# Output copies ahead of filter work at block seams, and a new order of the filter loads, in a fused FFT filter and SwiGLU kernel

**Chip and metric.** One core of a Trainium2 chip. The time is device microseconds (us) of the whole program, as the median of several executions. The engines are TensorE (PE in the profile), VectorE (DVE), ScalarE (ACT), GpSimd (POOL) and SyncE (SP), which here only issues DMAs.

## The reference

Each of 8 sequences (3008 x 256) goes through a Fourier filter, and all tokens then go through a gated feed-forward layer:

```python
X = np.fft.rfft(x, axis=1)
y = np.fft.irfft(X * (filt_r + 1j * filt_i)[None], n=x.shape[1], axis=1)
# ... tokens: y as (24064, 256)
rms = np.sqrt(np.mean(y * y, axis=-1, keepdims=True) + 1e-06)
xn = y / rms * rms_g
g = xn @ w_gate
out = ((g * sigmoid(g)) * (xn @ w_val)) @ w_out     # d_ff 1536
```

## The kernel before

The FFT is done by matmuls with small tables. The feed-forward layer is a chain of 588 *slots*: a slot computes 128 of the 1536 hidden columns for 512 tokens. Twelve slots are a *block*, whose result collects in the two PSUM banks `po`. The filter work of the next sequence is spread over the slots of the one before, by the lists `pre`, `plan` and `late`. Sequence 0 has nobody to hide behind: its filter work is the *head*, some 47 us.

```python
stores = {}
for i in range(len(items) + 4):
    for fn, a in pre.get(i, ()):       # second products ("swap") of a filter unit
        fn(*a)
    if i < len(items):
        gv(*items[i])                  # 4 matmuls of 512 columns, silu on ACT, hh = pv * sg on DVE
    for fn, a in plan.get(i, ()):      # filter units, first and last products, norms
        fn(*a)
    if 2 <= i < len(items) + 2:
        down(*items[i - 2])            # 4 matmuls of 256 columns; at a block's end the copies of po
        # ... (cut)
    for fn, a in late.get(i, ()):
        fn(*a)
    # ... (cut)
```

A block ends at slots 13, 25, 37 and so on (slot % 12 == 1): there `down` also copies one `po` bank on ACT and the other on DVE, and the next slot's `down` writes both banks anew. This is the *seam*.

A filter unit of sequences 1 to 7 uses one PSUM bank, `psb`, of which there is only one:

```python
ps = bank(3 if b else (0, 3, 4, 5)[i % 4], "psb")           # two matmuls into it
nc.vector.tensor_tensor(out=s1, in0=ps, in1=f1, op=ALU.mult)  # L252
# swap_unit, first half (L278), then second half (L276), the last reader of psb:
nc.vector.scalar_tensor_tensor(out=s2[a], in0=ps[e], scalar=-1.0, in1=f2[e], ...)
nc.vector.tensor_tensor(out=s2[a], in0=ps[e], in1=f2[e], op=ALU.mult)
nc.gpsimd.tensor_tensor(out=s, in0=s1, in1=s2, op=ALU.add)    # L282
# ... (cut: units of sequence 1 that are not summed have two full products, L268 and L269)
```

The start of the head loads `x` on GpSimd's DMA queue, then the two filters:

```python
for c in range(NXC):
    x_load(0, c)                               # 8 DMAs on the GpSimd queue
nc.gpsimd.memset(fi[0][HALF:P], 0.0)
nc.gpsimd.memset(fr[0][0:HALF], 0.0)
# ... (cut)
for c in range(4):
    f_load(c, 0, nc.sync)                      # real filter
    f_load(c, 1, nc.gpsimd if c < 3 else nc.sync)   # imaginary filter
```

## Time and profile before

| | before |
|---|---|
| median of the first 3 executions | 893.95 us (893.05 to 894.44) |
| profiled execution, span of the core | 890.6 us |
| TensorE busy | 873.5 us, 98% |
| first gate matmul (end of the head) | 47.15 us |
| TensorE's waits after that | 4.3 us |

The page's busy row says which engine is the bound; the table of waits says how much of it can be won; a timeline around each wait says which instruction stood in the way. These lines are in the prediction below.

### The profile page before, as it was taken

The numbers are of one execution on the slowest core, as the hardware profiler recorded it, in microseconds if no ns is written. First come the engines' busy times: TensorE is split into PE (matmuls) and PEld (weight loads), VectorE is DVE, ScalarE is ACT, GpSimd is POOL, SyncE is SP. The second block draws the span as 40 slices with busy tenths as digits, with TensorE's granted clock in tenths as the row PEclk, the third lists the DMA queues.
The fourth block names the chain that finished last, engine by engine and source line by source line (L and its number), as shares of the span: only waits on it lengthen the run. The fifth ranks groups of instructions, "written<-read, shape, count | busy, mean of one in ns | idle before, by whom it ended". The sixth has DMA issues, their size and how long they took to land.

```text
span 890.6 us, 17468 instructions
## 1 busy us (share of the span) xinstructions
PE 873.5 (98%) x6258; PEld 559.4 (63%) x6258; DVE 681.5 (77%) x1091; ACT 625.1 (70%) x1068; POOL 435.6 (49%) x392
## 2 busy tenths in 40 slices
PE   8799999999999999999999999999999999999997
PEld 5666666666666666666666666666666666666556
DVE  7866787889987877888688787888878887555555
ACT  7877657677677766877677766787657765676444
POOL 7843830656427661677236662376515762155300
PEclk9999999999999999999999999999999999999999
DMA  8696726675663456335645247233352232222202
GB/s 196 122 196 156 157 67 207 143 158 110 162 159 89 101 111 185 107 90 113 159 119 132 86 81 199 80 94 90 88 163 72 67 90 61 85 66 49 72 24 48
DMA packets 80095, 101.44 MB, mean 114 GB/s; under 512 B 8108, under 2 KB 56684, under 8 KB 79560
## 3 DMA queue, kind: packets, MB, share of 16 engines
q1 hardware_dynamic: 69688, 84.23, 34.8%
q0 software_dynamic: 10240, 15.96, 11.4%
q8 instruction: 49, 0.80, 0.4%
q14 instruction: 38, 0.31, 0.1%
q10 hardware_dynamic: 80, 0.13, 0.1%
HBM read 67.67 MB, written 46.78 MB: 129 GB/s over the span
## 4 chain that ended last, share of the span: by engine, by line
PE 87%; issue 4%; DVE 2%; ACT 2%; DMA 2%; POOL 2%; SPq 0%; ACTq 0%; POOLq 0%; DVEq 0%
PE po L462 26%; PE pg L443 25%; PE pv L443 25%; PE psi L291 3%; PE psb L238 3%; PE psn L323 2%; PE psa L203 2%; DMA fr<-in_filt_r_dram 1%; DVE o L469 1%; ACT fr L516 1%; DVE hh L448 1%; DMA rb<-r_tmp 1%; ACT gT L578 1%; PE psq L352 0%; POOL xc L188 0%
## 5 line engine op out<-in xcount | busy, mean ns | idle before, releaser
L448 DVE TENSOR_TENSOR hh<-pv,sg 128x512 f16<-128x512 f32 (+2 forms) x588 | 392.9, 670 | 190.2 <-ACT sg L447 77.6
L447 ACT ACTIVATE sg<-pg 128x512 f16<-128x512 f32 (+2 forms) x588 | 340.9, 580 | 227.5 <-PE pg L443 217.8
L462 PE MATMUL po<-wo,hh 128*128 128x256 f16 x2244 | 343.2, 272 | 3.8 <-DVE o L469 3.0
L443 PE MATMUL pv<-xn,wv 128*128 128x512 f16 (+2 forms) x1176 | 339.6, 370 | 0.0
L443 PE MATMUL pg<-xn,wg 128*128 128x512 f16 (+2 forms) x1176 | 339.5, 370 | 0.0
L462 PEld LDWEIGHTS <-hh 128*128 128x128 f16 x2256 | 216.4, 98 | 99.0 <-issue 5.3
L282 POOL TENSOR_TENSOR s<-s,s 128x512 f16<-128x512 f16 x102 | 117.9, 1157 | 237.5 <-DVE s L276 165.6
L443 PEld LDWEIGHTS <-wv 128*128 128x128 f16 x1176 | 114.9, 98 | 128.8 <-issue 0.3
L419 POOL TENSOR_TENSOR xn<-y,rb 128x1024 f16<-128x1024 f32 (+1 forms) x45 | 126.0, 2801 | 44.9 <-DMA rb<-r_tmp 37.7
L443 PEld LDWEIGHTS <-wg 128*128 128x128 f16 x1176 | 111.4, 98 | 13.0 <-issue 0.3
L358 POOL TENSOR_TENSOR rho<-u,mhalf 128x4 f32<-128x4 f32 (+1 forms) x48 | 49.1, 1022 | 63.5 <-DVE u L356 63.1
L276 DVE TENSOR_TENSOR s<-psb,fi 64x512 f16<-64x512 f32 x102 | 69.8, 684 | 3.1
L296 ACT ACTIVATE t<-psi 96x512 f16<-96x512 f32 x112 | 66.4, 593 | 8.1 <-PE psi L291 2.7
L278 DVE SCALAR_TENSOR_TENSOR s<-psb,fi 64x512 f16<-64x512 f32 x102 | 70.7, 693 | 1.4
L252 DVE TENSOR_TENSOR s<-psb,fr 128x512 f16<-128x512 f32 x102 | 69.4, 681 | 0.0
L329 ACT ACTIVATE y<-psn,gsb 128x512 f32<-128x512 f32 (+1 forms) x94 | 63.8, 679 | 7.8 <-PE psn L323 0.5
L343 POOL TENSOR_TENSOR sq<-sq 128x512 f16<-128x512 f16 (+1 forms) x35 | 39.6, 1133 | 35.9 <-ACT sq L335 35.9
L335 ACT ACTIVATE sq<-psn 128x512 f16<-128x512 f32 (+1 forms) x94 | 54.8, 583 | 0.0
L208 ACT ACTIVATE t<-psa 128x512 f16<-128x512 f32 x70 | 41.8, 597 | 5.6 <-PE psa L203 2.4
L291 PE MATMUL psi<-s,wi 128*128 128x256 f16 x236 | 44.1, 273 | 0.0
L238 PE MATMUL psb<-t,wb 96*128 96x256 f16 x224 | 43.0, 272 | 0.5 <-DVE s L269 0.5
L323 PEld LDWEIGHTS <-t 128*128 128x128 f16 x368 | 28.4, 98 | 20.6 <-issue 0.4
(104 smaller groups left out, 523.1 us busy)
## 6 DMA issues: line engine op xcount, KB each, us to landing
out_dram<-o SPq DMA_DIRECT2D x83, 256.0 KB
xc<-in_x_dram POOLq DMA_DIRECT2D x56, 192.0 KB, 5.8
z_tmp<-t SPq DMA_DIRECT2D x28, 384.0 KB
t<-z_tmp SPq DMA_DIRECT2D x28, 384.0 KB
g_tmp<-t SPq DMA_DIRECT2D x56, 192.0 KB
rb<-r_tmp SPq DMA_DIRECT2D x41, 256.0 KB
t<-g_tmp SPq DMA_DIRECT2D x21, 384.0 KB
t<-g_tmp SPq DMA_DIRECT2D x7, 320.0 KB
```

Of the source, the lines that this page charges most:

```text
L238: nc.tensor.matmul(ps[:, u, :], w[:, k, :], t, start=True, stop=True)
L252: nc.vector.tensor_tensor(out=s1, in0=ps, in1=f1, op=ALU.mult)
L276: nc.vector.tensor_tensor(out=s2[a], in0=ps[e], in1=f2[e], op=ALU.mult)
L278: nc.vector.scalar_tensor_tensor(out=s2[a], in0=ps[e], scalar=-1.0, in1=f2[e], op0=ALU.mult, op1=ALU.mult)
L282: nc.gpsimd.tensor_tensor(out=s, in0=s1, in1=s2, op=ALU.add)
L291: nc.tensor.matmul(ps[:, u, :], wi_at(q, 2 * i + u), ss[q][:, u, :], start=(q == 0), stop=(q == n - 1))
L296: nc.scalar.activation(out=st[b]["t3"][c][:, 2 * r:2 * r + 2, :], in_=ps[0:KR], func=AXT.Copy)
L419: nc.gpsimd.tensor_tensor(out=xv, in0=yv, in1=rv.unsqueeze(1).to_broadcast([P, 2, n, P]), op=ALU.mult)
L443: nc.tensor.matmul(ps[:, 0:w], wt[:, dt_, ts(jt, P)], xn[:, dt_, :], start=(dt_ == 0), stop=(dt_ == 1))
L447: nc.scalar.activation(out=sg[:, 0:w], in_=pg[:, 0:w], func=AXT.Silu)
L448: nc.vector.tensor_tensor(out=hh[:, 0:w], in0=pv[:, 0:w], in1=sg[:, 0:w], op=ALU.mult)
L462: nc.tensor.matmul(po[s4 // per][:, s4 % per, :], hh[:, ts(s4, P)], wo[:, jt, :], start=(jt == 0 and s4 % per == 0), stop=(jt == JT - 1 an ...
```

## The change

Its intent seems to be to take the waits at the seams away: at those slots products, evacuations and swap halves go after the output copies, one unit of sequence 1 goes a slot later, another unit's products go from DVE to GpSimd, one sum of squares is used a slot later, and the imaginary filter's first load is issued ahead of a memset.

```diff
-        return b > 1 or b == 1 and i in (6, 7, 10, 11, 14, 15)
+        return b > 1 or b == 1 and i in (6, 7, 10, 11, 14)
...
-        if (i in (3, 5, 8, 12)) if b else (i in (3, 7, 9, 12)):
+        if (i in (3, 5, 8, 12, 15)) if b else (i in (3, 7, 9, 12)):
             eng = nc.gpsimd
...
         nc.gpsimd.memset(fi[0][HALF:P], 0.0)
+        f_load(0, 1, nc.gpsimd)
         nc.gpsimd.memset(fr[0][0:HALF], 0.0)
...
-            f_load(c, 1, nc.gpsimd if c < 3 else nc.sync)
+            if c:
+                f_load(c, 1, nc.gpsimd if c < 3 else nc.sync)
...
-            todo = {q_unit: late, swap_unit: pre}.get(fn, plan).setdefault(slot, [])
+            at_seam = slot % JT == 1 and fn in (a_unit, b_unit, swap_unit)
+            todo = late if at_seam or fn == q_unit else pre if fn == swap_unit else plan
+            todo = todo.setdefault(slot, [])
...
-                r = (4, 8, 12)
+                r = (5 if (b, m) == (2, 1) else 4, 8, 12)
...
-                b_at = [22 + 7 * i // 4 for i in range(16)]
+                b_at = [22 + 7 * i // 4 + (i == 1) for i in range(16)]
```

## The prediction

> **What bounds the kernel now.** A slot is one gate/value group: four 512-column matmuls (gv), the slot's extra work, then the down projection of two slots earlier; 12 slots are a block, 6 blocks a sequence. I read the page first, then TensorE's (PE's) waits, then busy time by stretch, then timelines around every PE gap.
>
> ```profile
> PE 873.5 (98%) x6258; PEld 559.4 (63%) x6258; DVE 681.5 (77%) x1091; ACT 625.1 (70%) x1068; POOL 435.6 (49%) x392
> ...
> 80.00:140.00 60.00, 57.41 (x392) 36.51 (x390) 46.38 (x75) 38.05 (x66) 32.92 (x32) 1.00 0.53 116
> 300.00:600.00 300.00, 300.00 (x2066) 191.04 (x2065) 241.84 (x381) 220.23 (x378) 158.96 (x140) 1.00 0.48 120
> ```
>
> PE is the bound: 300.00 of 300 us busy late on (first busy column), 57.41 of 60 in the stretch where sequence 1 goes through the filter. Clock 1.00 throughout. So only PE gaps can be won. After the head (48 us) there is this, and nothing else:
>
> ```profile
> PE po L462 <- DVE o L469: 3.0, 6, 0.8
> PE psb L238 <- DVE s L269: 0.5, 2, 0.3
> PE psq L352 <- POOL sq L343: 0.5, 1, 0.5
> PE po L462 <- DVE hh L448: 0.3, 1, 0.3
> ```
>
> Some 4.3 us of 890: the ceiling is half a per cent. The first line is the seam: a block's last down projection (emitted at slot 12n+1) must be copied out of both po banks before the next block's first may write them (slot 12n+2), and VectorE's (DVE's) copy stands behind products. Seam at slot 25:
>
> ```profile
> 87.77 0.69 DVE L448 TENSOR_TENSOR hh<-pv,sg 128x512 f16<-128x512 f32 x1 [0.78 <-PE psb L238]
> ...
> 88.37 0.68 DVE L268 TENSOR_TENSOR s<-psb,fr 128x512 f16<-128x512 f32 x1
> ...
> 88.97 0.68 DVE L269 TENSOR_TENSOR s<-psb,fi 128x512 f16<-128x512 f32 x1
> ...
> 89.57 0.68 DVE L469 COPY o<-po 128x512 f32<-128x512 f32 x1
> ...
> 90.31 0.38 PE L462 MATMUL po<-wo,hh 128*128 128x256 f16 x2 [0.59 <-DVE o L469]
> ```
>
> Two products precede the copy; PE stands until 90.31. The printed 0.59 starts at a matmul's modelled end; from start to start (one 256-column matmul takes 0.108, a slot's gv 0.87, its down 0.43) the pause is 90.31 - 89.55 = 0.76. I use start-to-start values below.
>
> **What the Trainium skill says.** "PSUM — Partial Sum Buffer", Engine vs sequencer instructions: ScalarE, VectorE and GpSimd queues are strict FIFO. The trace agrees: the copy runs third, though po was ready before 88.4. So reordering moves waits and removes no work. "Perfetto Trace Analysis", Matmuls: independent matmul groups should rotate through PSUM banks so evacuation overlaps. Here psb has one bank, and the trace shows that: psb at 84.37 waits 0.29 for the previous unit's product. "GPSIMD Engine Reference", 4.1 Engine selection: two-input elementwise is about twice as slow there, and GpSimd has no PSUM port. Agrees: 1.27 us against 0.68, after a 0.58 us copy by ScalarE (ACT). "DMA: Bandwidth & Descriptors", Queues, rings and completion order: each DMA engine goes round-robin between its queues, so delaying one queue's entry hands its share to the other. The before-trace fits this (the filters start to move only as x drains), but no run isolates it yet.
>
> **Part by part: gains.**
> - Slot 25 (unit 2 after the copy) with unit 1 moved from slot 23 to 24. Before, slots 23 to 26 take 83.06 to 90.67 = 7.61 us. Without both waits I sum 6.74 (1.47 + 1.68 + 1.74 + 1.85, the third with a new 0.2 us wait for psb, since unit 1's products now end just before unit 2). Gain 0.87.
> - Slot 37, unit 9 behind the copy: pause 0.81 printed, 0.97 from start to start.
> - Slot 49: unit 15's two swapped products (0.69 + 0.68) stand before the copy; on GpSimd they leave DVE: 0.67 printed, gain 0.83. GpSimd is idle from 131.68 on, with 2 x 1.27 us to do before the unit's inverse at slot 52 (about 132.8): it should fit.
> - Slot 61, unit 11 of sequence 2's first products on DVE: 0.30 printed, 0.46. Slot 13: about 0.16, too short to be printed.
> - Sum of squares of sequence 2, block 1, one slot later, past the 1.16 us fold: 0.49 printed, 0.66.
> Sum 3.95 us.
>
> **Losses.** The rule also takes swap halves: sequence 2's units 0, 4, 8, 12 (slots 73, 85, 97, 109) and sequence 3's unit 0 (slot 121). There the second half (L276) frees psb, and the next unit's matmul wants psb in the very next slot. Seam at slot 85 before:
>
> ```profile
> 181.83 0.69 DVE L448 TENSOR_TENSOR hh<-pv,sg 128x512 f16<-128x512 f32 x1
> 182.56 0.68 DVE L276 TENSOR_TENSOR s<-psb,fi 64x512 f16<-64x512 f32 x1
> 183.27 0.69 DVE L448 TENSOR_TENSOR hh<-pv,sg 128x512 f16<-128x512 f32 x1
> 183.88 0.68 DVE L469 COPY o<-po 128x512 f32<-128x512 f32 x1
> 184.40 0.38 PE L238 MATMUL psb<-t,wb 96*128 96x256 f16 x2
> ```
>
> No pause here now. Afterwards the order is hh, hh, o, L276: the second hh starts once its silu is done (182.43 + 0.60, so about 183.08), the copy at 183.69, L276 at 184.29, ending 184.97; psb's matmul goes at 185.02 instead of 184.40: a new wait of 0.62. The same shift gives 0.58 at slot 97, 0.59 at 109. At 73 a psb wait of 0.89 replaces a po wait of 0.57; at 121, 0.82 replaces 0.43. Sum: 0.62 + 0.58 + 0.59 + 0.32 + 0.39 = 2.50 us.
>
> Unit 15 on GpSimd needs two products in its inverse instead of one sum: two more 256-column matmuls, +0.22 us.
>
> **Head.** Now the real filter's load waits in the sync queue for GpSimd's memset of fr (to 9.59), and the chain runs on it:
>
> ```profile
> SPq L503 <- POOL fr L655: 7.5, 1, 7.5
> ```
> ```profile
> 12.29 8.59 DMA fr<-in_filt_r_dram
> 20.99 1.16 ACT fr L516 x2
> ```
>
> The change puts four imaginary-filter issues before that memset; two of GpSimd's filter issues already wait for x to land (1.4 us in all), so I put the memset's end at about 13.8 and the real filter's entry 4 us later. But its packets do not move before about 13.7 anyway: x holds the DMA engines. They would begin near 15.2, yet the imaginary filter would by then be further along and compete less. Landing: 20.9, give or take 0.8. ACT is free at 20.61 and waited 0.37; it is 97% busy after that, so lateness passes to the end, earliness wins 0.37 at most. Mean of that: +0.25 us.
>
> **Sum:** -3.95 + 2.50 + 0.22 + 0.25 = -1.0. From 893.95: 892.9 us.
>
> **Rivals.** (1) Pure gain: psb frees in time at the five swap seams, perhaps because PE reaches them later, and the head is neutral: -3.7, 890.2. For it: the change was presumably meant so. Against: the DVE times above leave no slack, as the copy is held back by po itself. (2) The wait moves: psb waits come in full, and the head gives away more, say 1.5 us: -3.95 + 2.50 + 0.22 + 1.5 = +0.3, 894.2. For it: the real filter is on the chain at 12.29 to 20.88. Against: the DMA engines are shared, and its entry was not what held it. (3) GpSimd becomes the bound at slots 48 to 52: if its products end late, PE waits at the inverse, up to 1 us. Against: its timeline is idle there.
>
> **Range and chances.** The five seam estimates are one argument, so they fail together (2.5 us either way), and the head has 0.8 us; three runs of before spread over 1.4 us. 8 in 10: 890.7 to 895.0. A 2% change is 18 us, over four times all the pauses together: 98% same, 1% each side.
>
> **What would show it.** In PE's waits: "po <- DVE o" falls from 3.0 to under 0.5 us; a new row psb <- DVE s (L276) of about 2.5 us printed in five pieces up to 0.8; the psq row is gone. PE busy rises by 0.2 to 0.4 us. psi matmuls become 238. The chain's fr landing ends at 20 to 21.7, and slot 0 (first gate matmul, 47.15 now) moves by less than 0.8. The prediction is wrong if the psb row stays small (too high by 2.5), or if the filter lands beyond 22 (too low).

## The result

The changed kernel took 894.18 us (median of 4, 893.64 to 894.74) beside 893.5 us for the kernel before: a ratio of 1.0007, interval 0.999 to 1.0025. A second comparison with more executions (below) gave 1.0015, interval 1.0002 to 1.0028. The ratios are not quite the ratios of the medians. There is no gain; if anything the kernel is about 1 us slower.

TensorE's waits after the head, in the changed kernel (engine and line, what ended the wait, us in total, times, longest):

```profile
PE psb L238 <- DVE s L276: 3.3, 5, 0.8
PE po L462 <- DVE hh L448: 0.3, 1, 0.3
PE psb L238 <- DVE s L269: 0.2, 1, 0.2
```

The row "po <- DVE o" of 3.0 us is gone, and so is the psq row. A new row has come: the unit's matmul waits for `psb`, which the second swap half L276 frees. DVE's and PE's timelines of the changed kernel around the seam at slot 85, whose lines of before stand in the prediction:

```profile
181.92 0.69 DVE L448 TENSOR_TENSOR hh<-pv,sg 128x512 f16<-128x512 f32 x1
183.15 0.69 DVE L448 TENSOR_TENSOR hh<-pv,sg 128x512 f16<-128x512 f32 x1 [0.54 <-PE psi L291]
183.76 0.68 DVE L469 COPY o<-po 128x512 f32<-128x512 f32 x1
184.47 0.68 DVE L276 TENSOR_TENSOR s<-psb,fi 64x512 f16<-64x512 f32 x1
```
```profile
184.27 0.39 PE L323 MATMUL psn<-tb,t 128*128 128x128 f16 x4
185.21 0.38 PE L238 MATMUL psb<-t,wb 96*128 96x256 f16 x2 [0.55 <-DVE s L276]
```

The copy now goes before L276, as meant. But L276 ends at 185.15, and the next unit's matmul, which could have gone at about 184.5 (four matmuls of 128 columns after 184.27), goes at 185.21.

The other part is the head. The chain that ended last, in the changed kernel's first 25 us (start, duration, what):

```profile
11.32 0.55 POOL fi L510
11.91 1.81 POOL fr L656
13.73 0.94 SPq L503
...
16.42 6.07 DMA fr<-in_filt_r_dram
22.59 1.16 ACT fr L516 x2
```

Before, the memset of `fr` ended at 9.6 us and ACT took the real filter at 20.99; now the memset ends at 13.72 behind four DMA issues, and ACT takes the filter at 22.59. The first gate matmul came at 50.01 us instead of 47.15.

Reading the first gate matmul of every slot off both traces gives a ledger of the whole difference, in us from start to start (positive is slower):

| where | predicted | measured |
|---|---|---|
| head, to slot 0 | +0.25 | +2.86 |
| slot 13 | -0.16 | -0.17 |
| slots 23 to 26 | -0.87 | -0.99 |
| slot 37 | -0.97 | -0.97 |
| slot 49 | -0.83 | -0.83 |
| two more matmuls | +0.22 | +0.22 |
| slot 61 | -0.46 | -0.45 |
| seams 73, 85, 97, 109, 121 | +2.50 | +3.10 |
| sum of squares, block 1 of sequence 2 | -0.66 | -0.66 |

### The profile page after: what moved, and what is told of

Same layout as the page of the kernel before. It is cut to its first block, busy times and chain, and to the rows that moved or that the text cites. A ratio compares the mean times of both kernels' runs of the same rounds, so it can differ in the third digit from the quotient of the medians. Undisturbed runs are those within 1.5% of the kernel's fastest.

```text
span 892.6 us, 17472 instructions
## 1 busy us (share of the span) xinstructions
PE 874.7 (98%) x6260; PEld 560.7 (63%) x6260; DVE 679.5 (76%) x1088; ACT 625.8 (70%) x1069; POOL 436.5 (49%) x393
## 4 chain that ended last, share of the span: by engine, by line
PE 88%; issue 4%; DMA 2%; DVE 2%; ACT 2%; POOL 1%; SPq 0%; POOLq 0%; DVEq 0%; ACTq 0%
PE po L462 26%; PE pg L443 26%; PE pv L443 25%; PE psb L238 3%; PE psi L291 3%; PE psn L323 2%; PE psa L203 2%; DMA xc<-in_x_dram 1%; DVE o L469 1%; DMA fr<-in_filt_r_dram 1%; PE psq L352 0%; DVE s L276 0%; DMA rb<-r_tmp 0%; PE pt L589 0%; DMA r_tmp<-rho 0%
## 5 line engine op out<-in xcount | busy, mean ns | idle before, releaser
L443 PEld LDWEIGHTS <-wg 128*128 128x128 f16 x1176 | 111.3, 98 | 13.4 <-issue 0.3
L276 DVE TENSOR_TENSOR s<-psb,fi 64x512 f16<-64x512 f32 x101 | 69.0, 683 | 3.1
```

The lines of the kernel that those rows point to most:

```text
L443: nc.tensor.matmul(ps[:, 0:w], wt[:, dt_, ts(jt, P)], xn[:, dt_, :], start=(dt_ == 0), stop=(dt_ == 1))
```

## The experiments

All kernels gave correct results. Two numbers are read from each trace: the first gate matmul, which is the head's length, and the stretch from slot 0 to slot 146, in which all seam moves and the move of the sum of squares lie. That stretch was 228.91 us before and 228.13 in the changed kernel.

**Parts of the change alone.** Four kernels on one chip with 11 executions of before (median 893.9).

`head_only` is the kernel before with only the two edits of the filter loads:

```diff
         nc.gpsimd.memset(fi[0][HALF:P], 0.0)
+        f_load(0, 1, nc.gpsimd)
         nc.gpsimd.memset(fr[0][0:HALF], 0.0)
...
+            if c:
+                f_load(c, 1, nc.gpsimd if c < 3 else nc.sync)
```

> The kernel before with the filter loads' new order alone. My theory (the real filter's late entry is on the path): the first gate matmul comes some 1.5 to 3 us later than before's 47.15, real filter landing near 22.5 against 20.88, time +1.6 to +3 us; the rest of the trace as before. Part of the loss is a half-clock stretch of PE in the head, which may be there in some executions only. Rival (the head differed by chance between the two profiles): +0 +- 0.5 us and a landing near 21.

Measured: 895.13 us, ratio 1.0015 (0.9994 to 1.0036); real filter landing 23.37, first gate matmul 49.63, slot 0 to 146 228.91. The loss is in the head alone. By its time it is 1.2 to 1.3 us, less than the 1.6 to 3 expected, with an interval that just includes none.

`no_head` is the changed kernel with these two edits undone.

> The changed kernel with the filter loads back in the old order. My theory: first gate matmul near 47.2, time 2 to 3 us less than the changed kernel, so about 0.7 us less than before (gains 4.07, losses 3.10 + 0.22). Rival (head by chance): the same time as the changed kernel, within 0.5 us.

Measured: 892.65 us, ratio to before 0.9985 (0.9961 to 1.0009); first gate matmul 48.19, a microsecond over the expected 47.2 (the clock was halved for 3.41 us in this head too, see below); slot 0 to 146 228.14, as in the changed kernel. The direction and size of the time fit the theory; the interval does not exclude zero.

`swap_only` is the kernel before with the seam rule for the swap halves of sequences 2 and 3 only:

```diff
+            at_seam = slot % JT == 1 and fn == swap_unit and a[0] > 1
+            todo = late if at_seam or fn == q_unit else pre if fn == swap_unit else plan
```

> The kernel before with only the swap halves of sequences 2 and 3 put after the output copies at the five seams. My theory: psb waits for L276 of 3.3 us in five pieces, the po waits at slots 74 and 122 (0.40 + 0.26) gone, time +3.1 us from start to start. Rival (the waits are absorbed later, or come from the other moved parts): under +1 us.

Measured: 896.61 us, ratio 1.0031 (1.0009 to 1.0053); slot 0 to 146 231.99, that is +3.08. TensorE's waits after the head have the changed kernel's row:

```profile
PE psb L238 <- DVE s L276: 3.3, 5, 0.8
```

The five are 0.84, 0.55, 0.55, 0.55 and 0.78 us, at the five seams. The rival falls: the swap halves alone make these waits, and nothing absorbs them.

`no_swap` is the changed kernel with the old loads and without the swap halves in the rule:

```diff
-            at_seam = slot % JT == 1 and fn in (a_unit, b_unit, swap_unit)
+            at_seam = slot % JT == 1 and fn in (a_unit, b_unit)
```

> The changed kernel without the swap halves and without the filter loads' new order: the other seam moves alone. My theory: -4.07 + 0.22 = -3.85 us against before, PE waiting for o only at slots 74 and 122 (0.40 + 0.26 printed) and at 778, no psb wait on L276. Rival (the seam gains do not add up at the end): within 1.5 us of before.

Measured: 890.58 us, ratio 0.9966 (0.9942 to 0.9989); slot 0 to 146 225.04, that is -3.87 against the -3.85 expected (by its time, some -3.0). TensorE's waits after the head:

```profile
PE po L462 <- DVE o L469: 0.7, 2, 0.4
PE po L462 <- DVE hh L448: 0.3, 1, 0.3
PE psb L238 <- DVE s L269: 0.2, 1, 0.2
```

The other moves are worth what they take away, and no wait came in their place.

**What in the head costs.** The late entry of the real filter, or the early entry of the imaginary one?

`fr_first` swaps the two memsets of the kernel before, so that the real filter enters earlier.

> The kernel before with GpSimd's two memsets swapped, so that the real filter's load enters the sync queue near 7.8 instead of 9.6 us. Theory (before x has drained near 13.7 us the entry time does not matter; after it, it does): first real-filter packets still near 13.7, landing 20.5 to 21.3 as in the three other runs with the old order (ACT's copy of it at 20.99, 20.65, 20.63, 21.20), time within 0.6 us of before. Rival (every us of earlier entry is earlier landing): landing near 19, copy held only by ACT itself at 20.6.

Measured: 894.27 us, ratio 1.0003 (0.998 to 1.0026). My theory fell: the real filter's first packet moved at 11.92 us, not near 13.7 (13.48 to 13.74 in seven traces with the entry at 9.6), and it landed at 19.11, before the expected 20.5 (though four of those seven landed before 20.5 too, the earliest at 18.73, so the landing alone decides nothing). But the time did not fall. The likely reason is that `x` shares the engines and landed later. The start of this kernel's chain:

```profile
5.37 11.38 DMA xc<-in_x_dram
16.75 0.14 issue
16.88 0.49 PE pat L526 x6
```

Before, x was there at 15.18, and in the seven traces with the entry at 9.6 between 14.76 and 16.51, so 16.75 is late, but not by much more than chance gives. ACT's copy of the filter comes after a copy that hangs on x, so it went at 22.18 although the filter had long been there; the first gate matmul came at 49.58. This execution also had a half-clock stretch in its head (see below).

`fr_late` delays the real filter but leaves the imaginary one where it was, with a second memset of `fi` as the delay:

```diff
         nc.gpsimd.memset(fi[0][HALF:P], 0.0)
-        nc.gpsimd.memset(fr[0][0:HALF], 0.0)
+        nc.gpsimd.memset(fi[0][HALF:P], 0.0)
+        f_load(0, 1, nc.gpsimd)
+        nc.gpsimd.memset(fr[0][0:HALF], 0.0)
...
```

(Here and in `fi_early` the later loop leaves this load out, as in the changed kernel.)

> The kernel before with a second memset of fi ahead of the imaginary filter's first load, and that load ahead of the real filter's memset: the imaginary filter enters as in before (about 9.6 us) and only the real filter enters late (about 14 us). Theory (the real filter's late entry is the loss): as with the new order alone: landing 22 to 23.5, first gate matmul 1.5 to 3 us after 47.15, time +1 to +2 us. Rival (the imaginary filter's earlier entry takes the engines): landing near 21, time within 0.5 us of before.

Measured: 895.52 us, ratio 1.0022 (1.0007 to 1.0036); landing 23.94, first gate matmul 50.18.

`fi_early` is the opposite: the imaginary filter early, while the real filter's memset goes to DVE.

```diff
         nc.gpsimd.memset(fi[0][HALF:P], 0.0)
-        nc.gpsimd.memset(fr[0][0:HALF], 0.0)
+        f_load(0, 1, nc.gpsimd)
+        nc.gpsimd.memset(fr[3][0:HALF], 0.0)
...
-            nc.vector.memset(fr[c][0:HALF], 0.0)
+            nc.vector.memset(fr[c % 3][0:HALF], 0.0)
...
```

> The imaginary filter's first load as early as in the changed kernel, but the real filter's memset on VectorE instead (GpSimd takes that of the last filter chunk), so that the real filter enters near 8.4 us. Theory: landing 19 to 20.5, x landing late by up to 1.5 us (it shares the engines earlier), time within 0.7 us of before, not the +1.3 us of the changed order. Rival: the imaginary filter's early entry costs as in the changed kernel: landing over 22, +1 to +2 us.

Measured: 894.12 us, ratio 1.0007 (0.9992 to 1.0022); landing 18.71, x at 16.0, first gate matmul 49.03. So the two tests part the suspects: the real filter's late entry alone costs as much as the change's new order, and the imaginary filter's early entry costs nothing that can be told from noise. (The real filter entered 1.3 us earlier here than before, at 8.35; that this hides a cost is not excluded, but in `fr_first` an earlier entry alone won nothing.)

`after_again` is the changed kernel, in the same job.

> The changed kernel once more, more rounds, on one chip with the two head tests. Theory (gains 4.07, losses 3.1 at the swap seams, 0.22 of PE work, head 1.3 to 2): 0.3 to 1.2 us over before, clock of every run 0.998 or less, real filter landing 22 to 23.5. Rival (first comparison by chance): 0.5 to 1 us under before.

Measured: 895.46 us beside 893.62, ratio 1.0015 (1.0002 to 1.0028), clocks of 0.995 to 0.998, landing 23.04. By the medians more than I expected (1.8 us), by the ratio 1.3 us.

**A clock that halves in the head.** In the changed kernel's trace the granted clock falls for 3.41 us. Its busy time by stretch (PE's busy us first, the clock after POOL's figures):

```profile
24.00:28.00 4.00, 2.13 (x26) 1.64 (x27) 3.84 (x7) 3.93 (x5) 0.46 (x1) 1.00 0.79 161
28.00:32.00 4.00, 2.20 (x26) 1.47 (x23) 3.87 (x7) 3.95 (x7) 3.92 (x3) 0.99 0.67 154
32.00:36.00 4.00, 3.75 (x30) 2.99 (x31) 2.94 (x6) 2.69 (x6) 3.94 (x4) 0.58 0.44 92
```

PE is just over half busy from 24 to 32, waiting for DVE and ACT; then it runs at half speed until 35.34. The profiled execution of before had no such stretch, which made the comparison of the two profiles look worse (+2.86 us in the head) than the timed executions do.

Nine of the thirteen traces have one in the head, old loads or new, of 3.41 or 6.83 us. First gate matmul by its length (in `fr_first` the stretch came late, at 39.76):

| half clock in the head | real filter enters late | real filter enters at 9.6 or earlier |
|---|---|---|
| none | | before 47.15, `halves_early` 47.08, `late15` 47.42, `filler` 49.05 |
| 3.41 us | changed 50.01, `head_only` 49.63 | `no_head` 48.19, `no_swap` 48.82, `fr_first` 49.58 |
| 6.83 us | `after_again` 50.56, `fr_late` 50.18 | `swap_only` 48.25, `fi_early` 49.03 |

With the clock alike, late entry beside the old loads (`no_head` and `no_swap`, `swap_only`) costs 1.3 us in the second row and 2.1 in the third, from few traces. Over the three jobs, before was executed 33 times: the 14 executions with a clock of 0.999 or more took 892.7 us on average, the 16 with 0.997 or 0.998 took 894.2, the 3 lower ones 896.9. One stretch of 3.41 us at half clock lowers the mean by 0.5 x 3.41 / 890 = 0.002, so these groups are likely those with none, one and more; only profiled executions show it.

A low busy share alone does not decide it. Before kept its clock with little more:

```profile
24.00:28.00 4.00, 2.48 (x33) 2.03 (x33) 3.71 (x7) 3.93 (x6) 3.19 (x3) 1.00 0.85 181
28.00:32.00 4.00, 2.68 (x30) 1.98 (x31) 3.87 (x8) 3.95 (x7) 3.86 (x4) 1.00 0.62 135
```

`no_head`, with the same head, had 2.33 and 2.88 there and lost its clock at 30.06. What tips it is open.

`filler` puts four dummy matmuls instead of one ahead of each of sequence 0's units 4 to 15, in the kernel before:

```diff
-            nc.tensor.matmul(ps[:, 0, :], wz[:, 0:P], wz[:, 0:D], start=True, stop=True)
+            for _ in range(4):
+                nc.tensor.matmul(ps[:, 0, :], wz[:, 0:P], wz[:, 0:D], start=True, stop=True)
```

> The kernel before with four dummy matmuls instead of one ahead of each of sequence 0's filter units 4 to 15. Theory (in the head PE idles enough that in most executions its clock is halved for 3.41 us, which costs up to 1.5 us and makes the times spread): clock 0.999 or more in every run, no half-clock stretch in the head, first gate matmul 47 to 48, time 0 to 1 us under before and a smaller spread. Rival (dummies only lengthen the head): later first gate matmul by up to 1.5 us, same spread.

Measured: 894.12 us, ratio 1.0001 (0.9986 to 1.0016); the clock was 0.999 or 1.0 in all six executions, and they lie within 1.0 us. The same stretches:

```profile
24.00:28.00 4.00, 3.71 (x50) 3.35 (x48) 3.56 (x6) 3.93 (x6) 1.89 (x2) 1.00 0.77 188
28.00:32.00 4.00, 3.13 (x37) 2.37 (x35) 3.98 (x7) 3.95 (x6) 3.86 (x4) 1.00 0.64 133
32.00:36.00 4.00, 4.00 (x52) 3.62 (x50) 3.21 (x6) 3.14 (x7) 4.00 (x4) 1.00 0.18 39
```

Half of each theory held: with a busier PE the clock stayed, in all six executions, but the time did not fall. The first gate matmul came at 49.05, with x landing as late as 16.51 in that execution; how much of that is the dummies is not shown.

**A better kernel.** `halves_early` keeps the old loads and runs both swap halves of a seam's unit in the slot before the seam:

```diff
-                    at(s0 + 1 + (b > 1), swap_unit, b, i, 1)
+                    at(s0 + 1 + (b > 1 and (s0 + 2) % JT != 1), swap_unit, b, i, 1)
```

(In the seam rule swap halves count for sequence 1 alone, and of its units on DVE none has one at a seam here.)

> The seam moves without the swap halves' lateness; instead both halves of the five seam units run in the slot before the seam. Theory: no psb wait on L276 and no po wait at slots 74 and 122: against the run without swap halves another 0.57 + 0.43 = 1.0 us, so about 4.8 us under before. Rival (the earlier halves delay that slot's hh and PE waits there): no better than -3.3 us.

Measured: 889.86 us beside 893.52, ratio 0.9953 (0.9937 to 0.9969). In the trace the psb wait on L276 is gone, but slots 73 and 121 win 0.27 us together, not 1.0: at 161.88 a value matmul now waits 0.21 for the delayed hh, and at 237.50 a po wait of 0.12 is left. Slot 0 to 146 is 225.02, no better than `no_swap` (0.26 us were lost before slot 15 in this execution). So the rival holds for the larger part of that gain. That the time is lower than `no_swap`'s, measured in another job, is not explained by the seams; the head had no half-clock stretch in this profile.

`late15` also puts unit 15 back on DVE; by the same rule its halves go after the copy.

```diff
-        return b > 1 or b == 1 and i in (6, 7, 10, 11, 14)
+        return b > 1 or b == 1 and i in (6, 7, 10, 11, 14, 15)
...
-        if (i in (3, 5, 8, 12, 15)) if b else (i in (3, 7, 9, 12)):
+        if (i in (3, 5, 8, 12)) if b else (i in (3, 7, 9, 12)):
```

> The same with unit 15 back on VectorE, its two halves after the copy of seam 49, where no unit waits for psb. Theory: the seam at 49 is as free as with GpSimd, and two matmuls fewer: 0.22 us less than halves_early, PE 6258 matmuls. Rival (its sum comes late for the inverse at slot 52): a new PE wait of up to 0.7 us there.

Measured: 889.08 us, ratio 0.9959 (0.9936 to 0.9982; one execution at clock 0.992 took 894.7). It saved nothing: from slot 52 to 54 the trace is 0.30 us behind that of `halves_early`. I had overlooked that sequence 2's first products use the psb bank too:

```profile
129.75 0.68 DVE L276 TENSOR_TENSOR s<-psb,fi 64x512 f16<-64x512 f32 x1
...
130.49 0.38 PE L203 MATMUL psa<-xc,tb 128*128 128x512 f16 x1 [0.18 <-DVE s L276]
```

Both kernels beat the kernel before by about 4 us, and so the changed one by about 5 (worked out across jobs, not measured side by side); which of the two is better is open.

## Why the prediction was right or wrong

The predicted time was 892.9 us, in a range of 890.7 to 895.0; 894.18 lies in the range, and within 2% was right. The direction of the sum was not: -1.0 was forecast, +0.7 (and +1.3 by the ratio of the longer comparison) was measured. That the time fell in the range is due to the range's width: the head missed its own 0.8 us. Of the signs named, the po and psq rows behaved as said; the filter's landing at 22.48, beyond 22, and slot 0 moving by 2.86 instead of under 0.8 said that the head was wrong.

- **Gains at the seams: right.** 3.95 us were forecast, 4.07 measured. Shown by the ledger and by `no_swap`.
- **Losses at the five swap seams: mechanism right, size short.** 2.50 us were forecast, 3.10 measured, and `swap_only` showed them alone. I took 0.60 us from the start of the copy to the start of L276, as between the copy and an hh; the trace shows 0.71 (183.76 to 184.47). That is 0.1 us at each of the five. The Trainium skill has a model that fits ("VectorE: DVE Perf Modes", Two Vector instructions with no wait between them): an instruction whose operands start in another group of 32 partitions than those before is held until every earlier one has finished. L276's output starts at partition 64, the copy's at 0, and the trace agrees: L276 starts at 184.47, after the copy's end at 184.44, while the copy itself starts 0.08 us before the end of the hh in front of it. The prediction's own lines had it already: there L276 starts 0.73 us after the hh before it (181.83 to 182.56), and the next hh 0.71 after L276.
- **Two more matmuls: right**, +0.22.
- **Head: this step failed.** The prediction says that the real filter's "packets do not move before about 13.7 anyway" and "its entry was not what held it", and it put the landing at 20.9, give or take 0.8, for +0.25 us. Its entry is what held its start: with the entry at 7.77 and 8.35 the first packet came at 11.92 and 12.6, at 9.6 (seven traces) at 13.48 to 13.74, at 13.4 to 14.3 (four traces) at 16.06 to 16.39. That the filter began just as x drained was a coincidence of the kernel before, which I read as a cause; in `fr_first` and `fi_early` the filter began at 11.92 and 12.6 although x landed only at 16.75 and 16.0. Nor did the imaginary filter's lead buy the lateness back: the landing was 18.7 to 21.2 in the seven traces and 22.5 to 23.9 in the four. An earlier entry won nothing beside it: the two early ones landed at 19.11 and 18.71, about as the earliest of the seven (18.73). How much time that is: +1.2 to +1.3 by `head_only`'s time, +1.3 to +2.1 by the first gate matmul with the clock alike. (The mean of the changed kernel's two traces and `head_only`, 50.1, is 2.3 over that of six with the old loads, 47.8, but all three had a half-clock stretch and only three of the six.) Rival 2, which had +1.5 us for the head, was the nearest.
- **The half clock was not foreseen.** Lateness leaves PE idle longer, and the clock can fall on top. That the changed order makes the fall more frequent is likely, not shown: of its 16 executions (twice the changed kernel and `head_only`) none had a clock of 0.999 or more, of before's 33 there were 14, but on the chip of `head_only` only 2 of 11; `fr_late` had one of 4.

## What to carry to other kernels

Putting a copy ahead of a product moves the wait to whatever the product was to free: before reordering, list for each delayed instruction the buffer that it releases and who needs it next. With a single PSUM bank the next user is one slot away. And where two transfers share the DMA engines, that one starts to move when the other ends does not show that its entry time is free: delay or advance it once and measure the landing.

## What the Trainium skill lacked or had wrong

- "TensorE: Matmul & The Clock Gate", HAM oscillation, gives as the rule no PE-idle gaps over some 3.4 us, and in A second HAM failure mode that frequent micro-idles do it too, without a figure. Here the clock halved for 3.41 us after gaps of at most 1.13 us, with PE 2.13 and 2.20 of 4.00 us busy; filled to 3.71 and 3.13 of 4.00 it did not, and between (before, 2.48 and 2.68) it did not in the profiled execution, while `no_head` (2.33 and 2.88) lost it. A share of busy time is what the page lacks; these runs don't fix one either. Executions of before at a clock of 0.999 or more and at 0.997 or 0.998 differ by 1.5 us on average (892.7 and 894.2), more than the net effect of this change.
- "DMA: Bandwidth & Descriptors", Latency and other measured facts: some 600 ns to a hardware-queue DMA's first byte. In the loaded head the real filter's first packet came 4.1 us after its issue began (9.62 to 13.71), and 2.4 us in the changed kernel (13.73 to 16.15). The page has no first-byte figure under load; what made the two differ was not tested.
